# Postmix and product with v in 64x64 quadrants: one two-bank block for each group's maximum, transpose and rounding

## The chip, the cores and the metric

One core of one Trainium2 chip runs the whole kernel. The metric is the device time of one execution in microseconds. In the profile, PE is TensorE's matmuls, PEld its weight loads, DVE VectorE, ACT ScalarE, POOL GpSimd and SP SyncE, which here only issues DMAs. L540 is line 540 of the kernel before.

## What is computed

Attention whose scores are mixed over the heads before the softmax (premix) and once more after it (postmix), and a feed-forward layer with a rational activation on its result:

```python
batch, n_heads, seq, head_dim = (4, 12, 448, 64)
n_tokens, d_model, d_ff = (1792, 768, 2048)
scores = scale * np.matmul(q, k.transpose(0, 1, 3, 2))
scores = np.einsum('bhij,hg->bgij', scores, w_pre)
scores = scores - np.max(scores, axis=-1, keepdims=True)
attn = np.exp(scores)
attn = attn / (np.sum(attn, axis=-1, keepdims=True) + 1e-09)
attn = np.einsum('bhij,hg->bgij', attn, w_post)
x = np.matmul(attn, v)            # then reshaped to (1792, 768)
h = x @ w_in
g = (a[0] + a[1]*h + a[2]*h*h + a[3]*h**3) / (1.0 + np.abs(b[0])*np.abs(h) + np.abs(b[1])*h*h + 1e-6)
out = g @ w_out
```

The inputs are fp32. The feed-forward products split each fp32 value into a rounded part and a remainder (x, w and g each have a "hi" and a "lo" half).

## The kernel before

Each batch entry's 448 query rows are cut into four tiles, three of 120 rows and one of 88 (padded to 90), 16 tiles T in all. A tile holds 12 blocks of ten rows (9 in the short one), and two blocks make a group: six groups a tile, or five in the short one, the last with one block. There are 92 groups.

For a tile, `put_qk` (L463) makes the scores of a head pair: four 64x64 matmuls into two PSUM banks, two copies (ScalarE or VectorE) into `st`, and two DMAs (L489, the shuffle) that lay the rows of a head out in `d`, so that a partition holds one (row, head) pair. Twelve shuffles fill `d` for a tile.

For a group, `put_pre` (L524) mixes the heads with four 64x64 matmuls (L540) into two loose banks of the pool `ps_t` (four banks), takes the row maximum of each bank on VectorE (L547), exponentiates each bank on ScalarE with the sum as a by-product (L556), guards and inverts the sums (L563 on GpSimd, L567 on VectorE) and scales the postmix weights by them on GpSimd (`krs`, L576).

`put_post` (L599) stands two groups behind (`LAG` = 2): matmuls of 64x32 with 112 columns (L617) into the two banks of `ps_a`, and a 32x32-block transpose of each bank on VectorE (L633) into `aa`, where the keys of one head lie on partitions. When all groups of a tile are there, `put_av` (L665) multiplies with v: 24 matmuls of 128x64 with 120 columns (L676) for each half `hv` of the heads, into one bank of `ps_t`; ScalarE rounds the bank into `xs` (the hi part, `move` at L236), VectorE subtracts (L690, the lo part), and SP stores x (L694).

The order is made by a planner (`Plan`): each operation has an engine, a cost, dependencies and a due time `at`, and each engine's program is the resulting list. On TensorE the order of the attention work is that of the calls, since each of these operations may not start before the one before it (`pe`, L516). For group g the calls are: premix of g, early scores of the next tile, postmix of g - 2, a half of the product with v where one is due, late scores. Scores of head pairs 1 to 5 of tile T are put into the first four groups of tile T - 1 (three groups, if it has five): pairs 1, 2 and 3 early in groups 0, 1 and 2, pair 4 late in group 2, pair 5 early in group 3. The two halves of a product of tile T stand in groups `first[T + 1] + 2` and `+ 3`. `SLOT` and `HALF` (L290) are the spacing of the due times of groups.

The feed-forward stage (from L819) runs 64 units of two products, `m1` (L832) and `m2` (L921), with the activation between them on ScalarE, VectorE and GpSimd. Its first unit reads the last batch entry's x directly from `xs`.

Of the kernel before, what the change touches and what calls it, by code (L numbers as in the profile page):

```python
# [21 lines left out]
G5 = 5  # L22
# [7 lines left out]
NJ, JT = 4, 112  # L30
NB, BT = 7, 32
G6 = H // 2
# [209 lines left out]
def mixed_attention_then_rational_ffn(ctx: ExitStack, tc, q, k, v, w, wmix, mask, a, b2, out):  # L242
# [13 lines left out]
    ps = {n: ctx.enter_context(tc.tile_pool(name="ps_" + n, bufs=i, space=PSUM))  # L256
          for n, i in (("s", 2), ("t", 4), ("a", 2))}
    bank = lambda n: ps[n].tile([128, 512], F32, tag="b", name="ps_" + n)
    base, after = ctx.enter_context(ExitStack()), ctx.enter_context(ExitStack())
    left, right = ExitStack(), ExitStack()  # L260
    sb = {}

    def open_pools(stack, side, sizes):
# [9 lines left out]
        ("co", 2), ("ps_s", 2), ("ps_t", 4), ("ps_a", 2), ("a", 2), ("v", 2), ("xs", 1), ("xo", 2),  # L273
# [16 lines left out]
    SLOT, HALF = 3.85, 2.3  # L290
# [172 lines left out]
    def put_qk(T, pr, at, ps_="s"):  # L463
# [4 lines left out]
        def mm():  # L468
            box["s"] = [bank(ps_), bank(ps_)]
# [54 lines left out]
    def put_pre(g):  # L524
# [5 lines left out]
        box = [{} for _ in range(nt)]  # L530

        def pre():
            for r in range(nt):
                box[r]["t"] = bank("t")
# [9 lines left out]
        def top(r):  # L544
            def fn():
                nm = sb["e"].tile([128, 1], F32, tag="nm", name="nm")
                nc.vector.tensor_reduce(out=nm, in_=box[r]["t"][:, 0:S], axis=AX.X, op=ALU.max, negate=True)  # L547
                box[r]["nm"] = nm
            return fn

        def exp(r):
            def fn():
                e = sb["e"].tile([128, S], F32, tag="e", name="e")
                if r == 0:
                    box[0]["sm"] = sb["e"].tile([128, 2], F32, tag="sm", name="sm")
                nc.scalar.activation(  # L556
                    e, box[r]["t"][:, 0:S], AF.Exp, bias=box[r]["nm"], accum_out=box[0]["sm"][:, r:r + 1])
# [21 lines left out]
        slots = [R["ps_t"].take() for _ in range(nt)]  # L579
# [3 lines left out]
        os, prev = [], []  # L583
        for r in range(nt):
            o2 = add("dve", dve(S), top(r), [o, free[r]], at=at + 0.5 * r, after=prev[:])
            o3 = add("act", 0.84, exp(r), [o2], at=at + 0.5 * r, after=os[-1:])
            R["ps_t"].uses[slots[r].k].append(o3)
            os.append(o3)
            exps.append(o3)
            prev = [o2]  # L590
# [8 lines left out]
    def put_post(g, at):  # L599
# [5 lines left out]
        nt, m = len(box), nblk[T]  # L605
        banks = [{}, {}]

        def post():
            for c in range(2):
                banks[c]["p"] = bank("a")  # L610
# [10 lines left out]
        def turn(c):  # L621
            def fn():
                if kb == 0 and c == 0:
                    t = sb["a"].tile([128, NB * BT * (TI // G5)], F32, tag="a", name="aa")
                    A[T] = t.rearrange("q (b s p) -> q b s p", b=NB, p=BT)
                src = banks[c]["p"][:, 0:nt * NB * BT]
                if nt == 2:
                    o = A[T][:, :, kb + c:kb + c + m + 1:m, :].rearrange("q b r p -> q r b p")
                    src = src.rearrange("q (r b p) -> q r b p", r=2, b=NB)
                else:  # L630
                    o = A[T][:, :, c * m + kb, :]
# [430 lines left out]
```

## Time and profile before

| | |
|---|---|
| three runs | 877.32, 881.3, 882.75 us, median 881.3 |
| profiled execution | 876.83 us |
| its span, first to last instruction | 875.0 us |
| mean granted TensorE clock | 0.99 |
| TensorE, VectorE, ScalarE, GpSimd busy | 94%, 79%, 55%, 40% |
| attention until the first feed-forward matmul | 392.33 us |

The profile is of one execution. Busy time of an engine is the time in which one of its instructions runs; instructions of one engine can overlap at their ends. A wait in square brackets is the engine's idle time before the row and what released it, as inferred from semaphores. The ends of matmuls are modelled, so the distance from one block's start to the next one's is the better measure of what a block takes.

### The profile page before, as it was taken

What the parts mean: (1) busy time and instruction counts of PE and PEld (TensorE: products, weight loads), DVE (VectorE), ACT (ScalarE), POOL (GpSimd) and SP (SyncE); (2) the same over time, 40 slices, a digit from 0 to 9 for tenths busy, and PEclk for the clock granted to TensorE, in tenths of its full rate; (3) what the DMA queues carried; (4) which work ended last, traced back from release to release, by engine and by line L of the source; (5) the groups of instructions that cost most, each with busy time, mean ns of one, the idle gap of its engine ahead of it and who ended that gap; (6) DMA issues with size and microseconds to landing.
All of it is one profiled execution on the core that took longest, in us unless ns stands there. A gap on an engine that the chain in (4) does not pass through costs nothing.

```text
span 875.0 us, 27000 instructions
## 1 busy us (share of the span) xinstructions
PE 826.2 (94%) x11088; PEld 641.3 (73%) x11088; DVE 693.0 (79%) x1279; ACT 483.8 (55%) x1057; POOL 352.7 (40%) x476
## 2 busy tenths in 40 slices
PE   5699989999999899989999999999999999999996
PEld 1255545555555555678898898999999999999995
DVE  5587868797888787847889999999899898666664
ACT  2355656555565554426666566755665567445641
POOL 2234434534344342313545554655555554112111
PEclk9899999999999999999999999999999999999999
DMA  6677788768767863399263337654556653256314
GB/s 204 196 214 216 235 250 239 220 213 283 226 219 232 277 206 117 96 333 372 75 222 121 101 121 265 216 194 138 178 211 208 259 171 126 73 202 231 127 64 147
DMA packets 77548, 170.64 MB, mean 195 GB/s; under 512 B 13072, under 2 KB 54384, under 8 KB 76272
## 3 DMA queue, kind: packets, MB, share of 16 engines
q1 hardware_dynamic: 76824, 167.95, 59.2%
q8 instruction: 87, 1.43, 0.7%
q10 hardware_dynamic: 600, 0.97, 0.3%
q14 instruction: 37, 0.30, 0.1%
HBM read 90.86 MB, written 39.32 MB: 149 GB/s over the span
## 4 chain that ended last, share of the span: by engine, by line
PE 62%; DVE 14%; DMA 5%; issue 4%; ACT 2%; POOL 1%; SPq 0%; DVEq 0%; ACTq 0%; POOLq 0%
PE ps_s L832 19%; PE ps_t L921 13%; PE ps_a L921 7%; PE ps_t L676 7%; PE ps_a L617 6%; PE ps_t L540 5%; PE ps_s L473 5%; DMA d<-st 2%; DVE cg L406 2%; DVE rc L877 1%; DMA x_scr<-xs 1%; DVE cm L412 1%; DVE sq L865 1%; DVE rc L881 1%; DVE sq L874 1%
## 5 line engine op out<-in xcount | busy, mean ns | idle before, releaser
L921 PE MATMUL ps_t<-g,w 128*128 128x448 f32 x768 | 177.4, 366 | 0.9 <-POOL g L891 0.9
L921 PEld LDWEIGHTS ps_t<-g,w 128*128 128x128 f32 x768 | 144.0, 188 | 13.7 <-POOL g L891 1.7
L617 PEld LDWEIGHTS ps_a<-e,krs 64*32 64x32 f32 x5760 | 77.9, 106 | 83.1 <-issue 47.1
L556 ACT ACTIVATE e<-ps_t,nm 128x448 f32<-128x448 f32 x180 | 112.8, 634 | 42.6 <-DVE nm L547 37.1
L891 POOL TENSOR_TENSOR g<-rc,g 128x448 fp32r<-128x448 f32 x55 | 69.1, 1256 | 159.8 <-ACT g L236 88.5
L832 PE MATMUL ps_s<-x,w 128*128 128x448 f32 x576 | 122.5, 366 | 2.1 <-DVE m L861 2.1
L633 DVE STREAM_TRANSPOSE aa<-ps_a 128x448 f32<-128x448 f32 (+1 forms) x184 | 107.8, 618 | 20.8 <-PE ps_a L617 20.1
L832 PE MATMUL ps_s<-xs,w 128*128 128x448 f32 x576 | 122.5, 366 | 1.5 <-DVE m L861 1.5
L397 POOL TENSOR_SCALAR cm<-cm 128x384 f32<-128x384 f32 x64 | 99.5, 1560 | 58.7 <-ACT cm L392 58.6
L617 PE MATMUL ps_a<-e,krs 64*32 64x112 f32 x5760 | 105.5, 263 | 13.1 <-issue 9.5
L832 PEld LDWEIGHTS ps_s<-x,w 128*128 128x128 f32 x576 | 108.0, 188 | 11.7 <-DVE m L861 2.8
L832 PEld LDWEIGHTS ps_s<-xs,w 128*128 128x128 f32 x576 | 107.8, 188 | 11.6 <-DVE m L861 2.6
L473 PE MATMUL ps_s<-kk,q 64*64 64x448 f32 x720 | 98.5, 559 | 15.5 <-DMA q<-in_q 5.3
L547 DVE TENSOR_REDUCE nm<-ps_t 128x1 f32<-128x448 f32 x180 | 104.5, 607 | 7.3 <-PE ps_t L540 6.1
L576 POOL TENSOR_SCALAR krs<-kpost,rr 128x64 f32<-128x64 f32 x180 | 80.3, 461 | 69.5 <-DVE rr L567 55.0
L540 PE MATMUL ps_t<-d,kpre 64*64 64x448 f32 x720 | 93.4, 560 | 7.1 <-DMA x_scr<-xs 2.1
L921 PE MATMUL ps_a<-g,w 128*128 128x448 f32 x384 | 96.5, 366 | 0.0
L236 ACT COPY st<-ps_s 120x448 f32<-120x448 f32 (+1 forms) x101 | 51.3, 533 | 71.8 <-PE ps_s L473 37.3
L676 PE MATMUL ps_t<-aa,vv 128*64 128x120 f32 (+1 forms) x1536 | 84.9, 266 | 0.9 <-DVE aa L633 0.8
L428 POOL TENSOR_TENSOR w<-cm,w 128x384 fp32r<-128x384 f32 x48 | 60.1, 1252 | 57.7 <-ACT w L236 55.8
L845 ACT ACTIVATE m<-ps_s,a_sb 128x448 f32<-128x448 f32 x64 | 46.1, 720 | 67.3 <-PE ps_s L832 67.2
L676 PEld LDWEIGHTS ps_t<-aa,vv 128*64 128x64 f32 x1536 | 77.5, 138 | 6.7 <-issue 5.1
(60 smaller groups left out, 1070.3 us busy)
## 6 DMA issues: line engine op xcount, KB each, us to landing
d<-st SPq DMA_DIRECT2D x144, 210.0 KB
cr<-in_w SPq DMA_DIRECT2D x64, 384.0 KB
o_scr<-o SPq DMA_DIRECT2D x36, 448.0 KB
o<-o_scr SPq DMA_DIRECT2D x36, 448.0 KB
x<-x_scr SPq DMA_DIRECT2D x5, 2688.0 KB
xs<-x_scr SPq DMA_DIRECT2D x4, 2688.0 KB
d<-st SPq DMA_DIRECT2D x42, 157.5 KB
x_scr<-xs SPq DMA_DIRECT2D x12, 540.0 KB
```

The source lines that it names most:

```text
L397: nc.gpsimd.tensor_scalar(out=m, in0=m, scalar1=F64_MIN, scalar2=F64_MAX, op0=ALU.max, op1=ALU.min)
L473: nc.tensor.matmul(box["s"][hh][i0:i1, 0:S], lhsT=Q[T][d, pr, i0:i1], rhs=K[b][d, pr, :], start=True, stop=True)
L540: nc.tensor.matmul(box[r if nt == 2 else 0]["t"][64 * c:64 * c + 64, 0:S], lhsT=kpre[p], rhs=Dt[T][p, kb + c if nt == 2 else kb, :], start ...
L547: nc.vector.tensor_reduce(out=nm, in_=box[r]["t"][:, 0:S], axis=AX.X, op=ALU.max, negate=True)
L556: nc.scalar.activation(e, box[r]["t"][:, 0:S], AF.Exp, bias=box[r]["nm"], accum_out=box[0]["sm"][:, r:r + 1])
L576: eng.tensor_scalar_mul(box[r]["kr"], kpost, rr)
L617: nc.tensor.matmul(banks[c]["p"][BT * q_:BT * (q_ + 1), j0:j0 + JT], lhsT=box[r]["kr"][p, m_, :], rhs=box[r]["e"][p, q_ * JT:(q_ + 1) * JT ...
L633: nc.vector.transpose(o, src)
L676: nc.tensor.matmul(t[64 * hf:64 * hf + 64, pr * n:(pr + 1) * n], lhsT=V[b][:, j, g, :], rhs=A[T][:, 3 * (g // G6) + j, 0:n // G5, G5 * (g ...
L832: nc.tensor.matmul(h[:, 0:S], lhsT=W[fi][:, wi, kk * 128:(kk + 1) * 128], rhs=x[:, kk // 3, xj, kk % 3, :], start=(n == 0), stop=(n == 3 * ...
L891: eng.tensor_sub(g[:, 1, :], box["rc"], g[:, 0, :].bitcast(F32))
L921: nc.tensor.matmul(O[key][:, 0:S], lhsT=W[fi][:, wi, DM + m * 128:DM + (m + 1) * 128], rhs=box["g"][:, gi, :], start=(f == 0 and n == 0), ...
```

## The change

The postmix writes bank c of one two-bank block from row half c, with 224 columns a matmul: 16 matmuls for a group of two blocks in place of 32 with 112 columns. One transpose moves both banks, and `aa` is laid out by row, key block and head, so that its output is contiguous. The keys of v are laid out over two halves of the partitions (seven blocks of 32 keys in each half of the heads), without the overlap of zeros: 84 matmuls of 64x64 with 120 columns a tile in place of 48 of 128x64, in three calls, one for each pair of the heads, all in group `first[T + 1] + 2`. Their sums stand in both banks of one block, which is rounded by one cast and one subtraction. PSUM becomes four pools of two banks during attention: `ps_s` as before, and the pairs t, u and a. Groups take the pairs t and u in turn; a product takes the pair that the group before used, and the group after it stays on its own pair once more. The maximum of a group is one instruction over both banks. The feed-forward stage uses the same eight banks under other names.

```diff
-    SLOT, HALF = 3.85, 2.3
+    SLOT, HALF = 3.65, 2.2
...
-        def top(r):
-            def fn():
-                nm = sb["e"].tile([128, 1], F32, tag="nm", name="nm")
-                nc.vector.tensor_reduce(out=nm, in_=box[r]["t"][:, 0:S], axis=AX.X, op=ALU.max, negate=True)
-                box[r]["nm"] = nm
-            return fn
+        def top():
+            nm = sb["e"].tile([128, 2], F32, tag="nm", name="nm")
+            nc.vector.tensor_reduce(
+                out=nm[:, 0:nt], in_=box[0]["both"][:, 0:nt, 0:S], axis=AX.X, op=ALU.max, negate=True)
+            box[0]["nm"] = nm
...
             for r in range(nt):
-                for m_ in range(2):
-                    for q_ in range(NJ):
+                for jh in range(2):
+                    for m_ in range(2):
                         for c in range(2):
-                            p = slice(64 * c, 64 * c + 64)
-                            j0 = (2 * r + m_) * JT
+                            p, q_ = slice(64 * c, 64 * c + 64), BT * (2 * m_ + jh)
                             nc.tensor.matmul(
-                                banks[c]["p"][BT * q_:BT * (q_ + 1), j0:j0 + JT], lhsT=box[r]["kr"][p, m_, :],
-                                rhs=box[r]["e"][p, q_ * JT:(q_ + 1) * JT], start=True, stop=True)
+                                banks["p"][q_:q_ + BT, c, JH * r:JH * (r + 1)], lhsT=box[r]["kr"][p, m_, :],
+                                rhs=box[r]["e"][p, JH * jh:JH * (jh + 1)], start=True, stop=True)
...
+            nc.vector.transpose(
+                A[T][:, 2 * kb:2 * (kb + nt)].rearrange("q s b p -> q (s b p)"), banks["p"][:, :, 0:nt * JH])
...
-            for pr in range(3):
-                for j in range(NJ):
+            for j in range(NB):
+                for hv in range(2):
                     for hf in range(2):
-                        g = 2 * (3 * hv + pr) + hf
+                        p, g = slice(64 * hv, 64 * hv + 64), 2 * pr + hf
                         nc.tensor.matmul(
-                            t[64 * hf:64 * hf + 64, pr * n:(pr + 1) * n],
-                            lhsT=V[b][:, j, g, :],
-                            rhs=A[T][:, 3 * (g // G6) + j, 0:n // G5, G5 * (g % G6):G5 * (g % G6 + 1)],
-                            start=(j == 0), stop=(j == NJ - 1))
+                            box["x"][64 * hf:64 * hf + 64, hv, pr * n:(pr + 1) * n], lhsT=V[b][p, j, g, :],
+                            rhs=A[T][p, 0:n // G5, j, G5 * g:G5 * (g + 1)],
+                            start=(j == 0), stop=(j == NB - 1))
...
-            move(nc, eng, Xs[b][:, hv, 0, :, c0:c0 + r], box["t"])
+            move(nc, eng, Xs[b][:, :, 0, :, c0:c0 + r], part())
...
-            x = Xs[b][:, hv, :, :, c0:c0 + r]
-            nc.vector.tensor_sub(x[:, 1], box["t"], x[:, 0].bitcast(F32))
+            x = Xs[b][:, :, :, :, c0:c0 + r]
+            nc.vector.tensor_sub(x[:, :, 1], part(), x[:, :, 0].bitcast(F32))
...
     for T in range(NT):
-        for hv in range(2):
-            avs.setdefault(first[T + 1] - 1 + LAG + 1 + hv, []).append((T, hv))
-    for g in range(-1, len(groups) + LAG + 3):
+        for pr in range(3):
+            avs.setdefault(first[T + 1] + LAG, []).append((T, pr))
+    pairs, holds, other = {}, {}, {"t": "u", "u": "t"}
+    for g in range(len(groups) + LAG + 4):
+        now, kept = avs.get(g, ()), avs.get(g - 1, ())
+        pairs[g] = pairs[g - 1] if kept else other[pairs.get(g - 1, "t")]
+        for T, pr in now:
+            if pr == 0:
+                holds[T] = other[pairs[g]]
...
-    vt = np.zeros((B, NJ, NJ * BT, 2, G6, D), v.dtype)
+    vt = v.reshape(B, 2, G6, 2, NB, BT, D).transpose(0, 1, 3, 5, 4, 2, 6).reshape(B, 128, NB, G6, D)
```

## Rows read from the trace of the kernel before

**Rows 1.** The page's first part: busy us, share of the span, instructions.

```profile
PE 826.2 (94%) x11088; PEld 641.3 (73%) x11088; DVE 693.0 (79%) x1279; ACT 483.8 (55%) x1057; POOL 352.7 (40%) x476
```

**Rows 2.** Windows by stage: start:end and length, busy by engine, clock, DMA share, GB/s.

```profile
41.14:364.88 323.74, 306.38 (x7817) 181.89 (x7809) 257.13 (x553) 178.81 (x480) 131.12 (x273) 1.00 0.72 218
...
392.33:875.00 482.67, 470.46 (x2306) 431.90 (x2304) 397.87 (x655) 284.78 (x525) 203.89 (x151) 1.00 0.51 174
```

**Rows 3.** Timeline of PE over tile 14: start us, us, instruction, [idle before].

```profile
343.39 0.98 PE L540 MATMUL ps_t<-d,kpre 64*64 64x448 f32 x8
344.16 0.96 PE L473 MATMUL ps_s<-kk,q 64*64 64x448 f32 x8
345.06 1.08 PE L617 MATMUL ps_a<-e,krs 64*32 64x112 f32 x64
346.06 0.98 PE L540 MATMUL ps_t<-d,kpre 64*64 64x448 f32 x8
...
351.40 2.75 PE L676 MATMUL ps_t<-aa,vv 128*64 128x120 f32 x48
354.08 0.98 PE L473 MATMUL ps_s<-kk,q 64*64 64x448 f32 x8
...
355.74 1.07 PE L473 MATMUL ps_s<-kk,q 64*64 64x448 f32 x8
...
357.75 2.75 PE L676 MATMUL ps_t<-aa,vv 128*64 128x120 f32 x48
360.43 0.98 PE L540 MATMUL ps_t<-d,kpre 64*64 64x448 f32 x8
...
364.88 0.98 PE L540 MATMUL ps_t<-d,kpre 64*64 64x448 f32 x8
```

**Rows 4.** Windows: sum of the twelve first stretches, columns as above.

```profile
sum 156.27, PE 149.91 PEld 84.15 DVE 124.00 ACT 94.60 POOL 72.25; mean PE 12.49 PEld 7.01 DVE 10.33 ACT 7.88 POOL 6.02
```

**Rows 5.** Windows: one of the twelve second stretches, and their sum.

```profile
334.00:343.39 9.39, 9.35 (x276) 6.06 (x273) 7.21 (x17) 4.09 (x12) 1.96 (x6) 1.00 0.32 96
...
sum 122.79, PE 113.22 PEld 71.95 DVE 97.89 ACT 60.95 POOL 39.88; mean PE 9.43 PEld 6.00 DVE 8.16 ACT 5.08 POOL 3.32
```

**Rows 6.** Groups of instructions by form: busy us, mean ns | idle before.

```profile
L633 DVE STREAM_TRANSPOSE aa<-ps_a 128x448 f32<-128x448 f32 x176 | 105.0, 628 | 18.8 <-PE ps_a L617 18.1
L547 DVE TENSOR_REDUCE nm<-ps_t 128x1 f32<-128x448 f32 x180 | 104.5, 607 | 7.3 <-PE ps_t L540 6.1
...
L690 DVE TENSOR_TENSOR xs<-ps_t,xs 128x360 fp32r<-128x360 f32 x24 | 12.8, 533 | 32.7 <-ACT xs L236 32.7
...
L633 DVE STREAM_TRANSPOSE aa<-ps_a 128x224 f32<-128x224 f32 x8 | 2.8, 394 | 2.0 <-PE ps_a L617 2.0
```

**Rows 7.** Timeline of SP: the last two shuffles issued in tile 14.

```profile
357.58 1.61 SPq L489 DMA_DIRECT2D d<-st  x2
```

**Rows 8.** DMA traffic in 40 slices of 0.65 us from 340 to 366 us.

```profile
GB/s 30 38 0 0 0 0 63 174 163 113 21 168 138 177 39 190 141 141 25 182 146 149 44 0 0 0 143 146 180 138 163 146 97 6 0 0 0 0 25 0
```

**Rows 9.** Timeline of PE in tile 8: pair 5 of tile 9, tile 9's first premix.

```profile
217.95 1.07 PE L473 MATMUL ps_s<-kk,q 64*64 64x448 f32 x8
...
228.78 0.98 PE L540 MATMUL ps_t<-d,kpre 64*64 64x448 f32 x8 [2.11 <-DMA x_scr<-xs]
```

**Rows 10.** Windows: sum of the two tiles with five groups.

```profile
sum 44.68, PE 43.26 PEld 25.79 DVE 35.23 ACT 23.25 POOL 19.00; mean PE 21.63 PEld 12.90 DVE 17.62 ACT 11.63 POOL 9.50
```

**Rows 11.** Timeline in tile 14: the subtraction behind the first half of a product.

```profile
354.69 0.53 DVE L690 TENSOR_TENSOR xs<-ps_t,xs 128x360 fp32r<-128x360 f32 x1 [1.87 <-ACT xs L236]
```

**Rows 12.** Timeline where the feed-forward stage begins.

```profile
392.33 0.88 PE L832 MATMUL ps_s<-xs,w 128*128 128x448 f32 x3
392.45 0.38 ACT L236 CAST xs<-ps_t 128x264 fp32r<-128x264 f32 x1 [1.89 <-PE ps_t L676]
...
392.86 0.43 DVE L690 TENSOR_TENSOR xs<-ps_t,xs 128x264 fp32r<-128x264 f32 x1 [1.83 <-ACT xs L236]
```

**Rows 13.** Windows around two waits of TensorE; the clock is third from the end.

```profile
30.00:40.00 10.00, 4.55 (x103) 1.96 (x108) 3.67 (x8) 2.44 (x7) 2.17 (x6) 0.79 0.71 226
...
220.00:240.00 20.00, 17.89 (x498) 11.24 (x500) 15.97 (x36) 10.27 (x30) 7.78 (x18) 1.00 0.74 225
```

**Rows 14.** Timeline of PE: the end of the longest wait in attention.

```profile
37.77 1.77 PE L473 MATMUL ps_s<-kk,q 64*64 64x448 f32 x8 [5.30 <-DMA q<-in_q]
```

More of the change, by code (lines that the diff above doesn't have):

```diff
@@ L468, in mm @@
         def mm():
-            box["s"] = [bank(ps_), bank(ps_)]
+            if ps_ == "s":
+                box["s"] = [bank(ps_), bank(ps_)]
+            else:
+                pair = both(ps_)
+                box["s"] = [pair[:, 0], pair[:, 1]]
             for i0, i1 in ((0, 64), (64, TQ)):
@@ L530, in put_pre @@
         box = [{} for _ in range(nt)]
+        pair = pairs[g]
         def pre():
-            for r in range(nt):
-                box[r]["t"] = bank("t")
+            box[0]["both"] = both(pair)
+            for r in range(2):
+                if r < nt:
+                    box[r]["t"] = box[0]["both"][:, r]
             for c in range(2):
@@ L577, in norm @@
             return fn
-        slots = [R["ps_t"].take() for _ in range(nt)]
+        slots = [R["ps_" + pair].take() for _ in range(2)]
         free = [R["e"].take() for _ in range(nt)]
@@ L638, in put_post @@
         for u in e_use:
             u.append(o5)
-        for c in range(2):
-            deps, after = [o5], []
-            if kb == 0 and c == 0:
-                deps.append(R["a"].take())
-            else:
-                after.append(evac[T][0])
-            o6 = add("dve", dve(nt * NB * BT), turn(c), deps, at=at + 1.0, after=after)
-            R["ps_a"].uses[slots[c].k].append(o6)
-            evac.setdefault(T, []).append(o6)
+        deps, after = [o5], []
+        if kb == 0:
+            deps.append(R["a"].take())
+        else:
+            after.append(evac[T][0])
@@ L650, in put_v @@
+        o6 = add("dve", dve(2 * nt * JH), turn, deps, at=at + 1.0, after=after)
+        for slot in slots:
+            R["ps_a"].uses[slot.k].append(o6)
+        evac.setdefault(T, []).append(o6)
     def put_v(b, at, gap=8.0):
@@ L659, in put_v, with put_av @@
         v_ld[b] = []
-        for j in range(NJ):
-            v_ld[b].append(bulk(0.63, load(j), [free] + v_ld[b][:1], at=at + gap * j, nbytes=128 * H * D * 4, since=at + gap * j))
-    Xs = {}
-    def put_av(T, hv, at):
+        for i, j in enumerate(range(0, NB, 2)):
+            v_ld[b].append(bulk(
+                0.63, load(j), [free] + v_ld[b][:1], at=at + gap * i, nbytes=128 * min(2, NB - j) * G6 * D * 4, since=at + gap * i))
+    Xs, sums = {}, {}
+    def put_av(T, pr, at):
         b, n, r, c0 = T // 4, rows[T], real[T], row0[T]
-        box = {}
+        if pr == 0:
+            sums[T] = {}, [R["ps_" + holds[T]].take() for _ in range(2)]
+        box, slots = sums[T]
@@ L670, in mm @@
         def mm():
[L671 to L673 removed]
+            if pr == 0:
+                box["x"] = both(holds[T])
+            for j in range(NB):
+                for hv in range(2):
                     for hf in range(2):
[L675 removed]
+                        p, g = slice(64 * hv, 64 * hv + 64), 2 * pr + hf
                         nc.tensor.matmul(
[L677 to L680 removed]
@@ L693, in fn, with store @@
+        def store(hv, hl, cols):
             def fn():
```

129 lines of the change are left out of this document (59 added, 70 removed).

## The prediction

> **What bounds the kernel now.** I read the page's busy shares first, then the windows by stage, then TensorE's timeline over one tile, then the stretches of that timeline added over all tiles, and last the queue that issues DMAs. The span is 875.0 us, and TensorE is busy in 94% of it, VectorE in 79% [rows 1]. The windows split it [rows 2]: from 41.14 us, where tile 1's first premix starts, to 364.88 us, where tile 15's starts, TensorE works 306.4 of 323.7 us; the stage behind 392.33 us is the feed-forward part, which the change leaves alone but for bank names. So what the change saves on TensorE counts in full only where TensorE then waits for nothing else.
>
> TensorE's order in attention is fixed by the code, and one tile shows it [rows 3]: premix (343.39), scores of the next tile (344.16), postmix (345.06), next premix (346.06), a period of 2.67 us without a wait. Once a tile come two halves of the product with v, 2.68 us each (351.40 to 354.08 and 357.75 to 360.43). Between them stand the scores of head pairs 4 (354.08) and 5 (355.74). Pair 5 is the last work that the next tile's first premix (364.88) depends on: its two score banks are copied out, reshuffled by DMA into d, and that premix reads all twelve heads. I cut each tile there: a **first stretch** from its first premix to the scores of pair 5, and a **second stretch** from there to the next tile's first premix. Of the 14 tiles between 41.14 and 364.88, twelve have six groups: their first stretches add up to 156.27 us, mean 13.02 [rows 4], their second to 122.79 us, mean 10.23, of which 113.22 busy [rows 5]. A second stretch without a wait takes 9.39 us (334.00 to 343.39).
>
> **The change, part by part.**
>
> *Postmix.* Per pair of blocks 32 matmuls of 112 columns become 16 of 224. Each of the eight 64x32 parts of the array streams 448 columns either way. It takes 1.00 us now (345.06 to 346.06) where the premix, 448 columns in only four large matmuls, takes 0.77 (343.39 to 344.16) [rows 3]. Halving the instructions brings it near the premix; lower end 0.77, upper end 1.00, and I take 0.84, since it still changes the tiling on both sides. Saving 0.16 us a group.
>
> *Product with v.* Per tile 48 matmuls in two column halves (24 rounds of 120 columns) become 84 in four quadrants (21 rounds). Before, 12 rounds take 2.68 us, 0.223 a round [rows 3]; at that rate 21 rounds take 4.7 us, and at the premix's 0.77 us for 448 columns 21 x 120 columns take 4.3. I take 4.6 against 5.36: 0.76 us saved a tile. The v operand is now read in runs of five at seven times the distance; no row shows that stride, so its cost is bounded by nothing lost and by the two-at-a-time case among the rivals.
>
> These two make 6 x 0.16 + 0.76 = 1.7 us a tile, and over all 92 groups and 16 tiles 14 + 12 = 26 us, 33 if the postmix falls all the way to 0.77.
>
> *VectorE.* Two maxima of 607 ns become one over 896 columns, two transposes of 628 ns one of 896, two subtractions of 533 ns (360 columns) one of 720 [rows 6]. At 1.04 ns a column (628 less 394 ns for 224 columns more) the joined ones cost some 1.08, 1.10 and 0.91 us. That frees about 0.25 us a group, 22 us in all, on an engine that is not the limit: I count none of it. The price is delay: the first exponential waits for the joint maximum, some 0.45 us later than for one. Behind it are the guard, the reciprocal, the scaling on GpSimd and the postmix two groups later. The TensorE waits of the first stretches (156.27 less 149.91, 6.4 us in twelve) [rows 4] are such; I keep half, since the longer wait described next lets that chain catch up.
>
> *Where the product stands.* This is the part that I weigh most. Both halves used to stand in two groups, one ahead of the scores of pair 4 and one behind those of pair 5. Now all three parts stand in one burst ahead of pair 4. The first stretch becomes 12.35 (343.39 to 355.74) + 4.6 - 2.68 - 3 x 0.16 = 13.8, with waits 14.1. The second stretch loses its half: 9.39 - 2.68 - 3 x 0.16 - 0.1 (a tiling switch) = 6.1 us of TensorE work. In these 6.1 us the copies, four shuffles and their landing must fit, which had 9.39.
>
> They do not fit. In the lightest tile the last two shuffles are issued from 357.58 to 359.19, the second from about 358.4 on, 2.7 us after pair 5 began at 355.74 [rows 3, 7]; DMA traffic, in slices of 0.65 us from 340, falls to nothing in slices 33 and 34, about 361.5, 3.1 us later [rows 8]. With 0.8 us to the first premix, an estimate between nothing and the 3.3 us that are left to 364.88, that is 6.6 at least. In a loaded tile the premix at 228.78 came 2.11 us late, 10.83 us after pair 5's start at 217.95 [rows 9] (the profile names a store of x; the matmul reads only d). So the ends are 6.6 and, for a mean over tiles, 10.23. I take 8.3, just under their middle: the burst gives the DMA queue 2 us more to drain before pair 4. A tile then takes 14.1 + 8.3 = 22.4 against 13.02 + 10.23 = 23.25: 0.85 x 12 = 10.2 us gained.
>
> *Tiles with five groups* (two; 44.68 us together [rows 10]) have pair 5 ahead of both halves, so only the work counts: 1.5 us each, 3.
>
> *Banks.* Four loose banks become two pairs, and the product holds one pair from its first matmul to its subtraction. The group behind the burst reuses the pair of the group before; the burst itself (4.6 us) covers that. The second group behind it waits for the subtraction. That ends 1.14 us after the product today (354.08 to 355.22 [rows 11]); with casts and subtractions over both banks about 1.8, while 3.4 us of TensorE work lie between. Counted at nothing; without that cover it costs what the subtraction is late. The Trainium skill (Perfetto Trace Analysis, Optimizing Tensor Performance) says that independent matmul groups should rotate through different banks so that evacuation overlaps the next matmuls. By that rule the held pair costs a bubble in each tile, and the sum would be near zero; by the row it costs none. It stands as rival 3 below.
>
> *Ends.* Up to 41.14 us the kernel waits for loads: no change. At the far end the feed-forward stage starts at 392.33, as the product ends, though the second half's cast (392.45) and subtraction (392.86 to 393.29) come after, because the first half was ready [rows 12]. One cast and subtraction over both halves must now end first: +1.5 us, against 1.3 saved in the last two products. Zero. Loads of v are an eighth smaller, in a queue that is not full: zero.
>
> **Sum.** 10.2 + 3 = 13.2 us off the profiled execution's 876.8 us (875.0 span): 863.6. The median shown is 881.3, 0.5% above it, so 868 us. A measurement of this kernel can tell about 1% from no change, that is 8.8 us.
>
> **Rivals.**
>
> 1. *The shuffles are in time.* If the second stretch needs only the light tile's 6.6 us, a tile takes 20.7: 12 x 2.55 + 3 = 34 us, 848 us. For it: five of twelve second stretches show no wait today, as the one shown in [rows 5]. Against it: seven do, and DMA is 72% busy [rows 2].
> 2. *The shuffles eat it all.* At 9.4 us for the second stretch nothing is left: 876 to 886. For it: the mean today is 10.23 [rows 5].
> 3. *The held pair.* If the subtraction comes 1 us too late in each tile (1.6 us of slack and 1 more), the 13 us are gone: 881. For it: casts and subtractions queue behind other work on ScalarE and VectorE. Against it: the wait would stand inside the second stretch, where the shuffles are waited for anyway.
> 4. *Slower, by the clock.* The granted clock fell to its lower level (1.2 GHz) where TensorE had stood still 5.30 us for a load (mean 0.79 from 30 to 40 us: 2.1 us lost) and stayed at 2.4 GHz across the 2.11 us wait (1.00 from 220 to 240) [rows 9, 13, 14]. If shuffles stay as slow as in the stalled tile, 11 us, the wait is 11 - 6.1 = 4.9 us and the tile 25.1 long: 12 x 1.85 - 3 = 19 us lost without the clock, 895 to 910 with a dip of 2 us in some tiles. It decides from a second stretch over 9.4 us on.
> 5. *The quadrants do not run four at a time*, or the wide stride doubles a round: 9 us for the product, 3.6 more a tile, over 920. The premix is against it: four quadrants with 448 columns each end within 0.98 us [rows 3].
>
> **Chances.** Forecast (858 to 878) 0.44, of which 0.30 lies below 872.5; rival 1 0.24; rival 2 0.10; rival 3 0.04; rival 4 0.13; rival 5 0.05. Faster 0.30 + 0.24 = 0.54, same 0.14 + 0.10 + 0.04 = 0.28, slower 0.18. Range 850 to 890: rival 1 but for its edge, the forecast, rivals 2 and 3 whole. The likeliest case's own range is 858 to 878.
>
> **What would show it.** Postmix blocks of 0.8 to 0.9 us; one product burst of 4.4 to 4.8 us a tile; VectorE rows of about 1.1 us; and a wait of 1 to 4 us ahead of each tile's first premix, behind a DMA into d. If that wait is missing, rival 1 holds; if the granted clock dips between 41 and 365 us, rival 3. If bursts take 9 us, the product's price was wrong.

## The result and the profile after

The change made the kernel slower. Over 20 runs the changed kernel took a median of 887.6 us (880.4 to 896.6), and the kernel before, in 20 runs beside it, 879.2 (873.6 to 882.8). The ratio is 1.0078, with a 95% interval of [1.0055, 1.0102]; here and below a ratio leaves out runs in a slower state (over 1.5% above the fastest of the same kernel), so it need not be that of the medians. The forecast was 868 us and faster.

The profiled execution took 887.2 us, with a span of 885.4. The page's busy row of the changed kernel [rows 1]:

```profile
PE 811.3 (92%) x9360; PEld 604.2 (68%) x9360; DVE 670.2 (76%) x1062; ACT 492.2 (56%) x1058; POOL 357.6 (40%) x480
```

TensorE is busy for 14.9 us less and yet the span is 10.4 us longer. The windows by stage say where (columns as in [rows 2]): attention from tile 1's first premix to tile 15's, then up to the feed-forward stage, then that stage.

```profile
40.74:371.01 330.27, 292.00 (x6240) 149.65 (x6240) 239.18 (x366) 182.99 (x479) 131.62 (x277) 0.96 0.70 213
...
371.01:400.25 29.24, 21.84 (x588) 14.78 (x581) 17.12 (x27) 8.76 (x25) 10.18 (x32) 0.88 0.84 279
400.25:885.40 485.15, 471.94 (x2304) 431.67 (x2304) 391.97 (x640) 287.96 (x527) 206.18 (x153) 0.99 0.51 172
```

The attention stage is 6.5 us longer (330.27 against 323.74). TensorE is busy 14.4 us less in it and idle 20.9 us more, and the mean granted clock has gone from 1.00 to 0.96. The part up to the feed-forward stage gives 1.8 us more (27.45 before, between the two windows of [rows 2]), that stage 2.5, and tile 1 begins 0.4 us sooner: 10.4.

TensorE's timeline shows the new parts at work, first a product over 120 rows, then tile 12 [rows 3]:

```profile
126.71 4.67 PE L682 MATMUL ps_t<-aa,vv 64*64 64x120 f32 x168
131.14 0.99 PE L483 MATMUL ps_s<-kk,q 64*64 64x448 f32 x8
...
311.69 0.99 PE L627 MATMUL ps_a<-e,krs 64*32 64x224 f32 x32
312.61 3.23 PE L682 MATMUL ps_t<-aa,vv 64*64 64x90 f32 x151
316.50 0.55 PE L682 MATMUL ps_t<-aa,vv 64*64 64x90 f32 x17 [0.66 <-issue]
316.88 0.93 PE L483 MATMUL ps_s<-kk,q 64*64 64x448 f32 x8
317.62 0.93 PE L553 MATMUL ps_u<-d,kpre 64*64 64x448 f32 x8
318.49 1.41 PE L483 MATMUL ps_s<-kk,q 64*64 64x448 f32 x8
319.83 0.99 PE L627 MATMUL ps_a<-e,krs 64*32 64x224 f32 x32
...
328.08 0.98 PE L553 MATMUL ps_t<-d,kpre 64*64 64x448 f32 x8 [2.24 <-DMA x_scr<-xs]
```

A postmix takes 0.92 us to the next block (311.69 to 312.61), the undivided product 4.27 here, at 90 columns and with a wait of 0.66 us in it, and 4.43 at 120 (126.71 to 131.14). Pair 4 (316.88) and pair 5 (318.49) stand behind it, and the next tile's first premix waits. The twelve first stretches [rows 4] and the twelve second [rows 5], summed; two of each are shown:

```profile
77.07:88.98 11.91, 6.60 (x129) 2.69 (x129) 7.83 (x11) 6.27 (x19) 5.54 (x11) 0.96 0.84 250
...
88.98:105.62 16.64, 16.64 (x328) 8.75 (x328) 9.32 (x15) 7.91 (x20) 4.58 (x10) 0.82 0.57 152
...
363.39:371.01 7.62, 5.92 (x124) 2.10 (x120) 6.19 (x8) 4.49 (x13) 1.94 (x6) 1.00 0.28 87
...
349.55:363.39 13.84, 13.84 (x337) 8.02 (x329) 9.24 (x15) 7.89 (x21) 4.57 (x13) 1.00 0.32 98
...
sum 180.53, PE 173.07 PEld 98.25 DVE 115.81 ACT 96.87 POOL 72.84; mean PE 14.42 PEld 8.19 DVE 9.65 ACT 8.07 POOL 6.07
...
sum 108.14, PE 80.11 PEld 30.66 DVE 90.68 ACT 65.19 POOL 40.26; mean PE 6.68 PEld 2.55 DVE 7.56 ACT 5.43 POOL 3.35
```

First stretches: mean 15.04 us (before 13.02, forecast 14.1). Second: 9.01 (before 10.23, forecast 8.3). Read the two upper lines as a pair: a long second stretch (11.91) is followed by a long first one at a granted clock of 0.82. TensorE's timeline and the windows around that place show why:

```profile
83.14 0.99 PE L627 MATMUL ps_a<-e,krs 64*32 64x224 f32 x32
88.98 1.77 PE L553 MATMUL ps_t<-d,kpre 64*64 64x448 f32 x8 [4.85 <-DMA d<-st]
90.50 1.74 PE L483 MATMUL ps_s<-kk,q 64*64 64x448 f32 x8
...
95.98 0.99 PE L627 MATMUL ps_a<-e,krs 64*32 64x224 f32 x32
...
116.14 1.77 PE L553 MATMUL ps_u<-d,kpre 64*64 64x448 f32 x8 [2.36 <-DMA d<-st]
...
165.74 1.05 PE L553 MATMUL ps_u<-d,kpre 64*64 64x448 f32 x8 [3.49 <-DMA d<-st]
...
233.46 0.98 PE L553 MATMUL ps_u<-d,kpre 64*64 64x448 f32 x8 [1.71 <-ACT e L568]
```

```profile
80.00:88.00 8.00, 3.67 (x84) 1.58 (x80) 4.90 (x8) 4.29 (x13) 4.20 (x10) 1.00 0.81 234
88.00:94.80 6.80, 5.82 (x56) 2.00 (x60) 2.49 (x3) 1.78 (x5) 0.74 (x2) 0.50 0.40 104
94.80:102.00 7.20, 7.20 (x192) 4.25 (x188) 6.16 (x11) 4.84 (x13) 3.48 (x7) 1.00 0.56 162
```

TensorE stands still 4.85 us for a shuffle into d, and for 6.8 us its clock is at the lower of its two levels, 1.2 GHz; it works in 5.82 of them. The lower clock comes with the waits of 2.36 us at 116.14 and 3.49 us at 165.74 too (the first stretches that begin there have mean clocks of 0.82 and 0.90), and not with those of 1.71 us at 233.46 and 2.24 us at 328.08 (1.00 in both).

### The profile page after: what moved, and what is told of

Same layout as the page of the kernel before. It is cut to its first block, busy times and chain, and to the rows that moved or that the text cites. A ratio compares the mean times of both kernels' runs of the same rounds, so it can differ in the third digit from the quotient of the medians.

```text
span 885.4 us, 23186 instructions
## 1 busy us (share of the span) xinstructions
PE 811.3 (92%) x9360; PEld 604.2 (68%) x9360; DVE 670.2 (76%) x1062; ACT 492.2 (56%) x1058; POOL 357.6 (40%) x480
## 4 chain that ended last, share of the span: by engine, by line
PE 28%; DVE 25%; issue 6%; ACT 4%; DMA 3%; POOL 1%; SPq 0%; DVEq 0%; ACTq 0%; POOLq 0%
PE ps_s L846 9%; PE ps_t L935 3%; PE ps_u L935 3%; PE ps_a L935 3%; DVE sq L888 3%; DVE rc L895 3%; DVE rc L891 3%; DVE cg L412 3%; PE ps_a L627 2%; DVE o L972 2%; DVE sq L879 2%; DVE m L875 2%; DVE m L872 2%; PE ps_s L483 2%; PE ps_u L682 2%
## 5 line engine op out<-in xcount | busy, mean ns | idle before, releaser
L846 PEld LDWEIGHTS ps_s<-xs,w 128*128 128x128 f32 x576 | 107.6, 188 | 14.4 <-DVE m L875 4.2
L634 DVE STREAM_TRANSPOSE aa<-ps_a 128x896 f32<-128x896 f32 (+1 forms) x92 | 100.3, 1091 | 21.8 <-PE ps_a L627 21.4
L627 PE MATMUL ps_a<-e,krs 64*32 64x224 f32 x2880 | 93.6, 364 | 16.6 <-DVE aa L634 7.5
L627 PEld LDWEIGHTS ps_a<-e,krs 64*32 64x32 f32 x2880 | 45.3, 107 | 92.2 <-issue 41.2
L935 PE MATMUL ps_t<-g,w 128*128 128x448 f32 x384 | 96.5, 366 | 0.5 <-POOL g L905 0.5
L935 PE MATMUL ps_u<-g,w 128*128 128x448 f32 x384 | 96.4, 366 | 0.0
L935 PEld LDWEIGHTS ps_t<-g,w 128*128 128x128 f32 x384 | 72.0, 188 | 7.0 <-POOL g L905 0.9
L935 PEld LDWEIGHTS ps_u<-g,w 128*128 128x128 f32 x384 | 72.1, 188 | 6.1
L935 PEld LDWEIGHTS ps_a<-g,w 128*128 128x128 f32 x384 | 72.1, 188 | 6.0
L575 POOL TENSOR_SCALAR sm<-sm 128x2 f32<-128x2 f32 (+1 forms) x92 | 21.3, 232 | 126.7 <-ACT e L568 124.1
L568 ACT ACTIVATE e<-ps_t,nm 128x448 f32<-128x448 f32 x91 | 57.0, 633 | 21.0 <-DVE nm L559 13.0
```

The lines of the kernel that those rows point to most:

```text
L568: nc.scalar.activation(e, box[r]["t"][:, 0:S], AF.Exp, bias=box[0]["nm"][:, r:r + 1], accum_out=box[0]["sm"][:, r:r + 1])
L627: nc.tensor.matmul(banks["p"][q_:q_ + BT, c, JH * r:JH * (r + 1)], lhsT=box[r]["kr"][p, m_, :], rhs=box[r]["e"][p, JH * jh:JH * (jh + 1)], ...
L634: nc.vector.transpose(A[T][:, 2 * kb:2 * (kb + nt)].rearrange("q s b p -> q (s b p)"), banks["p"][:, :, 0:nt * JH])
L846: nc.tensor.matmul(h[:, 0:S], lhsT=W[fi][:, wi, kk * 128:(kk + 1) * 128], rhs=x[:, kk // 3, xj, kk % 3, :], start=(n == 0), stop=(n == 3 * ...
L935: nc.tensor.matmul(O[key][:, 0:S], lhsT=W[fi][:, wi, DM + m * 128:DM + (m + 1) * 128], rhs=box["g"][:, gi, :], start=(f == 0 and n == 0), ...
```

## Experiments

All ratios are to the kernel before, run beside. "Stage" is the time from tile 1's first premix to tile 15's in the profiled execution: before 323.7, after 330.3.

**1. Does the product's place do it?** Three kernels move work without changing it. Product one group later, behind pair 5:

```diff
-            avs.setdefault(first[T + 1] + LAG, []).append((T, pr))
+            avs.setdefault(first[T + 1] + LAG + 1, []).append((T, pr))
```

> The changed kernel with one edit: the whole product of a tile one group later, so that it stands behind the scores of head pair 5 and not ahead of pair 4. Theory A (the place of the product: the shuffles of pairs 4 and 5 no longer fit between pair 5 and the next tile's first premix): TensorE's own work in the second stretch goes from 6.1 to 10.7 us, more than the 9.0 us that the stretch takes now, so the waits in front of first premixes go, and with them the dips of the clock between 41 and 371 us; a tile takes about 20.6 us in place of 24.0, twelve tiles 41 us less: 842 to 858 us. Theory B (the new work itself is dearer: joint maximum and transpose, one pair of banks held, quadrants): the place does not matter, 878 to 892 us.

All pairs ahead of the product:

```diff
-(0, 2, 4, 5, 6) if n == 6 else (0, 1, 2, 3, 4)
+(0, 1, 2, 3, 4)
```

> The changed kernel with one edit: in tiles with six groups the scores of pairs 1 to 5 stand as in the tiles with five (pair 5 early in group 2, ahead of the product, pairs 2 and 4 late in groups 0 and 1). The product stays where it is. Theory A: the product now lies between pair 5 and the next first premix, 4.5 us more for the shuffles; 842 to 862 us, a little worse than the late burst, since ten score banks must be copied out in two groups. Theory B: 878 to 892 us.

The kernel before, with both halves of its product in the changed kernel's one place:

```diff
-            avs.setdefault(first[T + 1] - 1 + LAG + 1 + hv, []).append((T, hv))
+            avs.setdefault(first[T + 1] + LAG, []).append((T, hv))
```

> The kernel before with one edit: both halves of its product in one group, ahead of pair 4, all its arithmetic, banks and orders else as they were. Theory A: the second stretch has 6.7 us of work left where the shuffles need about 9, the first one grows by 2.7; a tile goes from 23.25 to about 24 us, and waits of 3 us and more halve the clock for a while: 885 to 903 us, slower than before by 1 to 2.5%. Theory B: the place alone changes nothing, 874 to 884 us.

Measured: 1.0023 [0.9984, 1.0062], 1.0170 [1.0072, 1.0268] and 1.0139 [1.0065, 1.0212]; stages 330.2, 333.2 and 336.2. The third is clear: the one place alone, with old matmuls, makes the kernel 1.4% slower, so the place is enough for a loss like the change's. That the new operations cost nothing it does not show. The other two fell against the theory (medians 883.0 and 896.6 us): with pair 5 ahead of the product the waits for shuffles shrink, but others come. TensorE's waits from 41 to 368 us with the product behind pair 5 (us in total, times, longest):

```profile
PE ps_s L483 <- DVE st L238: 5.9, 6, 2.0
PE ps_u L553 <- DVE xs L697: 4.8, 4, 1.2
...
PE ps_t L553 <- DMA d<-st: 4.3, 2, 2.4
PE ps_t L553 <- DVE xs L697: 3.9, 4, 1.2
```

The held pair, rival 3, now costs 8.7 us (4.8 + 3.9), where it costs 2.4 in the changed kernel.

**2. What does the clock cost?** Twelve extra matmuls into the pair that the premix is about to overwrite, ahead of each tile's first premix, keep TensorE at work while it waits.

```diff
+            for _ in range(3 if kb == 0 and T > 1 else 0):
+                for c in range(2):
+                    for r in range(2):
+                        p = slice(64 * r, 64 * r + 64)
+                        nc.tensor.matmul(
+                            box[0]["both"][64 * c:64 * c + 64, r, 0:S], lhsT=kpre[p],
+                            rhs=K[T // 4][p, c, :], start=True, stop=True)
```

> The changed kernel with twelve matmuls more (three rounds of four quadrants, 448 columns each, about 2.4 us) right ahead of each first premix from tile 2 on, into that premix's own banks, which it then overwrites: TensorE works in most of the wait for the shuffles. They are thrown away; the result is unchanged. If the clock is part of the loss, its mean over 89 to 371 us goes back to about 1.00 and the sum of the first stretches falls by 6 to 10 us, while second stretches whose wait was shorter than 2.4 us grow by up to 13 us together: 878 to 892 us in all. If the clock is not part of it, the first stretches stay as long as they are (mean 15.0 us), and the time rises to 893 to 900 us.

Measured: 1.0201 [1.0125, 1.0278]. Its stage, then the sums of its first and second stretches:

```profile
39.92:378.88 338.96, 316.06 (x6576) 158.39 (x6580) 240.74 (x368) 183.36 (x480) 132.76 (x280) 1.00 0.68 208
```

```profile
sum 169.61, PE 164.78 PEld 93.98 DVE 107.69 ACT 94.65 POOL 68.15; mean PE 13.73 PEld 7.83 DVE 8.97 ACT 7.89 POOL 5.68
...
sum 122.16, PE 107.88 PEld 41.91 DVE 98.43 ACT 68.49 POOL 45.83; mean PE 8.99 PEld 3.49 DVE 8.20 ACT 5.71 POOL 3.82
```

The clock stays at 1.00, and the first stretches fall from 180.5 to 169.6 us: the lowered clock, and a wait in a burst told of at the end (4.12 us), are worth 10.9 us. The filler itself adds 14 us to the second stretches, also where there was no wait, and 5.6 to the two five-group tiles. So as a remedy it loses: 896.5 us, above the 892 expected.

**3. Is it the landing of the shuffles?** Half the columns in each shuffle, and nothing else, in the changed kernel, in the one before, and with the product behind pair 5:

```diff
-out=Dt[T][p0:p0 + STRIDE * (G10 - 1) + 1:STRIDE, 0:nblk[T], :], in_=box[h % 2][0:n])
+out=Dt[T][p0:p0 + STRIDE * (G10 - 1) + 1:STRIDE, 0:nblk[T], 0:S // 2], in_=box[h % 2][0:n, 0:S // 2])
```

> The changed kernel in which each shuffle carries only half of the columns (the rest of the rearranged scores stays as it was cleared, so part of the computation is left out). Nothing else moves. Theory A, the shuffles land late and their lateness is what costs: the waits in front of the premixes that end with a transfer (6.8 + 5.5 + 2.2 us in the changed kernel) go, and with them the lowered clock behind three of them (6.8 + 6.8 + 3.4 us at half speed, worth 8.5), in all some 23 us: 860 to 870 us. Theory B, the landing is not what holds the attention stage, and the waits only move to another releaser: 878 to 892 us.

> The kernel before with the same halved shuffles (the same part of the computation left out): the control. Its premixes wait 4.2 us in all for transfers, so both theories expect little: 873 to 882 us. If it falls below 870, the shuffles slow more than the premixes that wait for them.

> The changed kernel with its product with v one group later, behind the scores of pair 5, and with halved shuffles (part of the computation left out). That placement alone gave 883 us, with only 4.3 us of waits for shuffles in the attention stage, but longer stretches behind pair 5. Theory C, a tile's transfers take their 24 us whatever TensorE does: with half of the bytes it falls to 845 to 862 us. Theory D, in this placement other waits hold it (the copies that free the banks of the scores, 5.9 us; the subtraction that frees the held pair, 8.7 us): 876 to 884 us.

Measured: 0.9667 [0.9591, 0.9743], 0.9697 [0.9615, 0.9778] and 0.9726 [0.9647, 0.9805]; stages 302.0, 310.8 and 309.4. All three fall, by 2.7 to 3.3%, 24 to 29 us. The control fell too, against both theories; some 7 us of that lie ahead of tile 1's first premix (34.1 us for 41.1). But the stages now stand the other way round: after 8.8 us shorter than before.

These halves held zeros in half of the premix's operand. The next two keep real scores there (whole shuffles for tiles 0 and 1, `w_ = S if T < 2 else S // 2` for the width):

> The changed kernel; shuffles whole for tiles 0 and 1 and of half the columns from tile 2 on (so part of the computation is left out), the other half keeps the real scores of tiles 0 and 1, not zeros. If the gain of 30 us from halved shuffles came from fewer bytes: nearly all of it stays, less what the halved start gave (tile 1's first premix came 9 us sooner): 852 to 866 us. If it came from the zeros that half of the premix's columns held: 878 to 890 us.

> The kernel before with the same edit (the same part left out). Fewer bytes: 855 to 868 us, with an attention stage from tile 1's to tile 15's first premix some 9 us longer than the changed kernel's. Zeros: 875 to 885 us.

Measured: 0.9732 [0.9692, 0.9772] and 0.9777 [0.9734, 0.9819]. It is the bytes, not the zeros. Fewer bytes also lighten the DMA engines for every other transfer (a share of 0.58 and 0.59 in the stage, for 0.72 and 0.70), so these runs do not tell a shuffle's own time from the traffic beside it. The stage and the sums of first and second stretches, for the kernel before with halved shuffles:

```profile
40.35:351.24 310.89, 303.25 (x7817) 181.84 (x7809) 256.07 (x553) 178.66 (x481) 131.67 (x274) 0.99 0.58 172
...
sum 156.09, PE 150.26 PEld 84.99 DVE 128.05 ACT 99.53 POOL 76.22; mean PE 12.52 PEld 7.08 DVE 10.67 ACT 8.29 POOL 6.35
...
sum 113.18, PE 111.48 PEld 71.30 DVE 92.87 ACT 56.09 POOL 36.33; mean PE 9.29 PEld 5.94 DVE 7.74 ACT 4.67 POOL 3.03
```

and for the changed kernel:

```profile
38.23:339.93 301.70, 281.82 (x6241) 145.42 (x6241) 238.17 (x366) 183.54 (x481) 133.02 (x278) 1.00 0.59 177
...
sum 169.11, PE 164.49 PEld 94.75 DVE 122.60 ACT 103.76 POOL 83.38; mean PE 13.71 PEld 7.90 DVE 10.22 ACT 8.65 POOL 6.95
...
sum 91.29, PE 78.79 PEld 30.18 DVE 81.88 ACT 57.55 POOL 30.46; mean PE 6.57 PEld 2.51 DVE 6.82 ACT 4.80 POOL 2.54
```

This is the core of the case. With early shuffles the change shortens the stage by 9.2 us (310.89 to 301.70), with whole ones it lengthens it by 6.5. Whole shuffles cost the kernel before 9.6 us in its second stretches (113.18 to 122.79), 3.1 in its two five-group tiles (41.62 to 44.68) and nothing in the first stretches; they cost the changed kernel 16.9 us in the second (91.29 to 108.14), 0.3 in the five-group tiles (41.30 to 41.60) and 11.4 in the first stretches (169.11 to 180.53), where the clock is low. Of these last, 5.9 lie in tile 10 (20.66 us for 14.79), whose product stops with no transfer named.

In the whole time the turn is smaller: the change is 0.8% slower with whole shuffles, and with halved ones its ratio is 0.3 and 0.5% below that of the kernel before, with overlapping intervals. In the last pair of profiles 5.0 us of the stage's 9.2 are lost again between tile 15's first premix and the feed-forward stage (32.45 us for 27.44), and 2.9 in that stage.

The queue's part was tried by having ScalarE issue the loads of q, k and v:

```diff
-            nc.sync.dma_start(out=Q[T], in_=q[T])
+            (nc.scalar if T > 1 else nc.sync).dma_start(out=Q[T], in_=q[T])
...
```

> The changed kernel with the loads of q, k and v (from the second tile or batch on) issued by ScalarE and no longer by SP, so that shuffles don't stand behind them in SP's queue; the same bytes move. Theory A in the form 'queueing behind bulk': the waits for shuffles in front of the premixes fall from 12 to some 4 us and most of the lowered clock behind them goes: 868 to 878 us. If the shuffles are slowed by what all transfers share, whichever engine issues them: 882 to 892 us. If the issues delay ScalarE's exponentials and copies: over 892 us.

Measured: 1.0256 [1.0154, 1.0358], stage 350.5 at a clock of 0.94, with single waits of up to 7.1 us ahead of first premixes. Taking q, k and v out of SP's queue helps nothing. The time lies where late exponentials and copies were expected, but that ScalarE was late is not shown. Nor does the run settle queueing: the loads and stores for w and the stores of x still stand in SP's queue, and ahead of the wait of 7.1 us (from 231 to 246 us) SP itself stood idle before a shuffle:

```profile
SPq L500 <- DMA kk<-in_k: 4.2, 1, 4.2
```

The Trainium skill (DMA: Bandwidth & Descriptors, Issuing engines are not separate DMA queues) says that transfers end up on the same 16 DMA engines whichever engine starts them, and interleave. This run fits that and does not prove it.

**4. Can the shuffles be relieved?** Conversions of w later, towards the light last tiles:

```diff
-at=T0 + 30.0 + (tau[first[NT - 1]] - T0 - 60.0) * i / (PH * NCV))
+at=T0 + 100.0 + (tau[first[NT - 1]] - T0 - 100.0) * i / (PH * NCV))
```

> The changed kernel with the sixteen conversions of w (each loads 384 KB and stores 384 KB) begun 70 us later and spread up to the last tile, so that the loaded tiles 2 to 5 lose that traffic and the light last tiles get it; all work is kept. Theory A (late landing of shuffles, made late by the bulk traffic beside them, costs the time): the waits in front of the premixes of tiles 3 and 4 (4.9 and 2.9 us) and the lowered clock behind them (3.4 us each) go, worth 12 to 15 us of 887: 868 to 877 us. If the later tiles become loaded instead and wait in their turn: 880 to 892 us.

> The kernel before with the same later conversions of w. Its premixes wait little for transfers (4.2 us in all), but with halved shuffles it also fell by 30 us, of which some 10 ahead of tile 1. Expected from a lighter middle part: 872 to 882 us. If it gains as much as the changed kernel does, the traffic holds both alike and doesn't explain why the change made it slower.

Pair 4 ahead of the product, alone and with the later conversions:

```diff
-(0, 2, 4, 5, 6) if n == 6 else (0, 1, 2, 3, 4)
+(0, 2, 3, 4, 5) if n == 6 else (0, 1, 2, 3, 4)
```

> The changed kernel with the scores of pairs 3 and 4 of the next tile one place sooner, so that pair 4 stands ahead of the undivided product and only pair 5 behind it (in the changed kernel two pairs, four shuffles, stand behind it; moving the whole product behind pair 5, or all five pairs ahead, gave 883 and 897). Theory A: two shuffles less in the rush behind the product, and pair 5 lands 0.9 us sooner; of the 12 us of waits for shuffles two thirds go, and half of the lowered clock: 870 to 879 us. If the waits only move to the banks of the scores and to the copies: 881 to 897 us.

> Both edits together: pair 4 ahead of the product, and the conversions of w later. Theory A: the gains add as far as waits are left, 860 to 873 us, under both kernels. Otherwise no better than the better of the two alone.

Measured: 1.0114 [1.0022, 1.0205], 1.0001 [0.9962, 1.0040], 0.9996 [0.9949, 1.0042] and 1.0088 [1.0052, 1.0123]. Moving bulk traffic in time moves the waits with it (in the changed kernel the second stretches of tiles 1 and 10 now take 11.9 and 11.0 us, for 8.4 and 8.7). With two shuffles fewer behind the product alone, the loss does not show in the ratio, and the stage is 10.2 us shorter than the changed kernel's (320.1). It is not clear of noise: the ten runs spread from 875.6 to 890.9 us with a median of 885.8, against 881.9 of the kernel before, and the two kernels that have this edit beside others (1.0088 here, 1.0107 below) stay slower.

**5. VectorE's joined operations and the end.** Two maxima for the joint one; and a kernel with that, pair 4 ahead, and the last postmix but one in the pair of its own group's scores:

```diff
...
-        o2 = add("dve", dve(nt * S), top, [o, free[0]], at=at)
         for r in range(nt):
+            o2 = add("dve", dve(S), top(r), [o, free[r]], at=at + 0.5 * r)
```

```diff
...
+        where = pairs[g] if g == len(groups) - 2 else "a"
...
-            banks["p"] = both("a")
+            banks["p"] = both(where)
...
```

> The changed kernel with two maxima of one bank each for the joint maximum (0.607 us each before, 1.05 us joint), the first exponential waiting for the first alone. If the longer chain from premix to postmix costs, through the waits of postmixes for krs and the reciprocal (6.2 and 2.2 us) and the exponentials (3.0 us): 2 to 8 us off, 879 to 886 us against 888. If the 0.16 us more of VectorE in each of 90 groups weighs more: 888 to 896 us.

> Pair 4 ahead of the product (that alone: ratio 0.9996 to the kernel before), two maxima, and the last group but one's postmix in the pair of banks that its own scores leave free, so that the last groups don't pass through one pair. If the three add up: 3 us at the end and 2 to 8 from the maxima off 882: 871 to 879 us, 0.4 to 1.2% under the kernel before. If the waits move to the joint transpose (13.2 us with pair 4 ahead): 880 to 890 us.

Measured: 1.0101 [1.0044, 1.0158] and 1.0107 [1.0057, 1.0158]. Neither gains: giving up the joint maximum does not lower the time, and the end did not become shorter (33.5 us from tile 15's first premix to the feed-forward stage, for 29.2 in the changed kernel).

**6. The new product, divided over two groups.** One or two of its three parts behind pair 5:

```diff
-            avs.setdefault(first[T + 1] + LAG, []).append((T, pr))
+            avs.setdefault(first[T + 1] + LAG + (pr > 0), []).append((T, pr))
```

> The changed kernel with the product's first third (some 1.5 us) in its present group and the other two (3 us) one group later, behind the scores of pair 5; the held pair is held for one group longer, so that three premixes in a row share the other pair. Theory A (the burst between the scores makes the shuffles late): pair 5's scores come 3 us sooner after the tile's first premix, 11 for 14 us, the waits of the premixes for shuffles go, and the attention stage from tile 1's to tile 15's first premix falls from 330 to 310 to 318 us: 868 to 876 us. If the shared pair makes premixes wait for exponentials instead: 880 to 892 us.

and with `(pr > 1)`:

> The same with two thirds in the present group and one behind pair 5. Theory A: pair 5 comes 1.5 us sooner than in the changed kernel, half of the waits go: 875 to 882 us. If the shared pair costs more than the waits: 882 to 892 us.

Measured: 0.9943 [0.9904, 0.9982] and 0.9923 [0.9875, 0.9971]: both beat the kernel before, by 0.6% and 0.8%, with medians of 876.5 and 870.9 us, just above the first forecast and below the second. The theory had expected a stage of 310 to 318 us for the first; it is 322.0, and 322.7 for the second. With one part behind pair 5:

```profile
sum 155.40, PE 152.53 PEld 77.67 DVE 112.55 ACT 89.82 POOL 72.88; mean PE 12.71 PEld 6.47 DVE 9.38 ACT 7.49 POOL 6.07
...
sum 125.56, PE 96.77 PEld 47.89 DVE 100.09 ACT 68.38 POOL 41.07; mean PE 8.06 PEld 3.99 DVE 8.34 ACT 5.70 POOL 3.42
```

Together 281.0 us, against 288.7 in the changed kernel and 279.1 before. In the second stretches 28.8 us are still waits (125.56 less 96.77). Its profiled execution took 876.6 us where the median of its five is 870.9, so that the trace does not show where the gain of the times lies.

## Why the prediction was wrong, point by point

- **Postmix and product.** Right in sum: 0.92 us for 0.84 forecast (1.00 before, and with the switch of tiling in it), so half of that saving, and 4.43 for 4.6. TensorE's work in the stage fell by 21.4 us where no shuffle was late (303.25 to 281.82, halved shuffles). Rival 5 is out.
- **First stretch, forecast 14.1.** Right without late shuffles: 169.11 / 12 = 14.09. With them it was 15.04. The 0.94 us by twelve, 11.3 us, comes from the lowered clock behind three late shuffles (first stretches of 16.64, 16.72 and 16.96 us, for 13.9 without a wait) and from tile 10 (20.66), where the wait described below stands in the product. The sum had priced the clock in rival 4 alone and left it out of the forecast, though the forecast itself expected waits of 1 to 4 us. That is the first step that failed.
- **Second stretch, forecast 8.3.** Mis-sized: 9.01, so 8.5 us over twelve tiles. The shuffles are late in loaded tiles (11.91 us in the one shown), as forecast. But the lower bound of 6.6 us was read as the shuffles' own, and it is not: the light last tile takes 7.62, takes the same with halved shuffles (second row), and its end shows a postmix that waits for `krs` (1.01 us) and a premix right behind the postmixes, with no wait for a shuffle:

```profile
369.62 0.61 PE L627 MATMUL ps_a<-e,krs 64*32 64x224 f32 x16 [1.01 <-POOL krs L588]
...
371.01 0.98 PE L553 MATMUL ps_t<-d,kpre 64*64 64x448 f32 x8
```

```profile
332.31:339.93 7.62, 5.92 (x124) 2.11 (x121) 6.18 (x8) 4.48 (x13) 1.94 (x6) 1.00 0.15 45
```

  With halved shuffles the mean is 7.61 (91.29 / 12): a floor that the postmix's chain sets and that the forecast did not have. The shuffles add 1.40 us a tile to it. That the burst lets the DMA queue drain, on which the 8.3 leaned, no run shows by itself. These two terms make 11.3 + 8.5 = 19.8 us and turn 10.2 us gained into 9.6 lost; with the 3.1 gained in the five-group tiles and 3.9 lost outside the stage that is the span's 10.4.
- **Rival 4** is the one that came about, below its own price (895 to 910 us, with a wait of 4.9 us in every tile). It was to decide from a second stretch of 9.4 us on, priced as if all tiles were alike. The mean stayed at 9.01, but the waits are uneven: four of twelve stretches passed 9.4, and three of those made the next first stretch 2.7 to 3.1 us longer, most of it by the lower clock.
- **Five-group tiles.** The size was right, 41.60 us against 44.68, the reason was not: with halved shuffles it is 41.30 against 41.62. What these tiles gained is not work but the cost of whole shuffles, 3.1 us there in the kernel before and 0.3 in the changed one.
- **Held pair, counted at nothing.** Nearly right in this place: 2.4 us of waits for the subtraction in the stage. The Trainium skill's rule (Perfetto Trace Analysis, Optimizing Tensor Performance: independent groups rotate through banks) is right where the cover is gone: 8.7 us with the product behind pair 5.
- **VectorE, counted at nothing.** The joined operations take 1.07, 1.11 and 0.90 us, as worked out; they free 0.29 us a group by these figures, not 0.25. But they, and the chain behind them, cost TensorE time. With halved shuffles TensorE stands idle 12.2 us longer in the stage than before (301.70 less 281.82, against 310.89 less 303.25), and most of it is ahead of postmixes. Their rows in the stage, with halved shuffles, before and after:

```profile
L618 PE MATMUL ps_a<-e,krs 64*32 64x112 f32 x5160 | 91.4, 262 | 6.9 <-issue 4.8 <-DVE aa L634 1.4
L628 PE MATMUL ps_a<-e,krs 64*32 64x224 f32 x2576 | 82.0, 356 | 13.0 <-POOL krs L589 5.5 <-DVE aa L635 5.1 <-DVE rr L580 1.9
```

  The waits for `aa` are for the transpose that frees the one pair of the postmix; the others fit faster work that catches up with the chain behind it. Half of the first stretches' 6.4 us of waits was to go; 4.6 are left (169.11 less 164.49). In the second stretches, where the forecast had a wait for shuffles alone, they came to 12.5 us (91.29 less 78.79), for 1.7 before (113.18 less 111.48). It is why only 9.2 of the 21.4 us of saved work are gained in the stage even with early shuffles. Two maxima did not change the time; the joint transpose alone was not tried.
- **Ends, counted at zero.** 1.8 us too long up to the feed-forward stage. The last postmixes follow each other at 2.4 to 3.4 us, the product behind them waits 0.80 us for a transpose, and the first feed-forward matmul waits 0.73 for the cast over both halves. With halved shuffles this part is 2.6 and 5.0 us longer than in the kernel before (28.13 for 25.57, 32.45 for 27.44), so the term is mis-sized in every pair. The 2.5 us of the feed-forward stage stay open: over all kernels run here it took 480.2 to 487.0 us.

## What to carry to other kernels

Work saved on the busiest engine is lost if it shortens the time that a transfer had to land in: add up, per period, what must land between the last producer and the first reader, and halve the bytes once to see what the landing costs. A wait is not paid once: price the lower clock behind it, from the uneven waits, not from their mean. Take the floor of a stretch from every chain that ends in it: here the postmix's chain held it at 7.6 us, not the shuffles. The same burst moved apart around the critical producer (two parts ahead, one behind) measured 0.8% under the kernel before, where one burst measured 0.8% above; why it gains, its trace does not show.

## What the runs showed of the hardware

In the changed kernel's attention stage the lower clock came with waits of 4.85, 3.49 and 2.36 us for shuffles, the last with two short waits just ahead of it (0.26 and 0.23 us), and not with those of 2.24 and 1.71; the length of the one wait hardly tells the last two cases apart. One such fall had no transfer behind it: in tile 10 the product stops in its middle, with no releaser in the profile, and the clock is 0.50 for 6.8 us from 268.90 on:

```profile
263.75 2.47 PE L682 MATMUL ps_u<-aa,vv 64*64 64x120 f32 x84
270.33 2.87 PE L682 MATMUL ps_u<-aa,vv 64*64 64x120 f32 x50 [4.12 <-issue]
```

```profile
268.90:275.70 6.80, 5.37 (x68) 4.21 (x72) 0.76 (x2) 1.29 (x2) 0.23 (x1) 0.50 0.31 97
```

A packet of the instruction queue lies in that stop, between 267.7 and 267.9 us. That the burst waited for instructions fits, but the execution has 74 packets of that queue, and no run took it apart. Nor was it expected that half of the shuffles' bytes cost the kernel before some 20 us (0.9777 of 880.7), though only 4.2 us of waits for transfers stand ahead of its premixes from tile 1 on.
